# Sinkhorn block attention followed by a token mixer: a staged kernel becomes one software pipeline over batches

## The chip, the core and the metric

The kernel runs on one core of a Trainium2 chip. The core has a matrix engine (PE, whose weight loads the profile lists as PEld), a vector engine (DVE), a scalar engine (ACT), GpSimd (POOL), and a queue engine (SP) that here only issues transfers. PE writes to PSUM alone; DVE and ACT copy from there to the on-chip SBUF; transfers go over 16 DMA engines. The metric is device time in microseconds (us) for one execution; smaller is better.

## The reference

There are 4 batches, 8 heads, 768 tokens, 64 elements a head. An 8 x 8 matrix P for each batch and head is normalised five times (exponential, rows, columns). It mixes the 8 blocks of 96 tokens of K and of V. Then each block of Q attends to the mixed block at its own place. The heads side by side form x, 768 x 512, which goes through a mixer without softmax.

```python
    for _ in range(5):
        P = P - np.max(P, axis=-1, keepdims=True)
        P = np.exp(P)
        P = P / (np.sum(P, axis=-1, keepdims=True) + 1e-09)
        P = P / (np.sum(P, axis=-2, keepdims=True) + 1e-09)
    ...
    k_sorted = np.einsum('bhij,bhjcd->bhicd', P, k_b).reshape(B, H, S, D)
    v_sorted = np.einsum('bhij,bhjcd->bhicd', P, v_b).reshape(B, H, S, D)
    ...
    W_tok = scale * np.einsum('bsd,btd->bst', wq, wk)
    mixed = np.einsum('bst,btd->bsd', W_tok, x)
    return (np.maximum(mixed, 0.0) @ w_out).astype(np.float32)
```

Here wq and wk are x times two 512 x 64 weights. The kernels form wk transposed times x first (64 x 512, "Ab"), then wq times it.

## The kernel before

The instructions of each engine are ordered by the framework's scheduler. The work has three stages.

*Sinkhorn* (lines 59 to 77): 32 matrices on 32 partitions, eight small DVE operations and one exponential on ACT an iteration. P transposed goes to DRAM (L77).

*Two groups of two batches* (loop at L93). A partition is one block of one head, 128 in all, and holds its 96 x 64 elements in one row. Sixteen small transfers (L97) read P back into a block-diagonal 128 x 128 matrix, `lhsT`. Q, K and V come in over POOL's queue with a cast to bf16 (L106, L110). K and V are multiplied by `lhsT`, 512 columns at a time (L113), and copied out of PSUM by ACT (L115) and DVE (L123). PE then transposes Q, K and V in pieces of 128 x 64 or 128 x 96 (L145, L160), up to 32 into one PSUM tile. One copy of up to 4096 elements a partition takes each tile out, reading with a stride (L154, L169). Attention (L172 to L205) takes four heads of a block at a time: four score matmuls (L180), one exponential (L186), four matmuls with V (L190), whose 65th column of ones gives the row sum, a reciprocal (L198) and a product (L205). The result goes to DRAM (L208).

*Mixer* (loop at L232), one batch at a time: x is read back twice, transposed (L236) and plain (L242). Then come wq (L249), wk (L257), Ab (L265), the mixing with ReLU (L274 to L277) and the output product (L283), copied by ACT or DVE (L286) and stored on SP's queue (L287).

Of the kernel before, what the change touches and what calls it, by code (L numbers as in the profile page):

```python
# [17 lines left out]
def kernel(  # L18
# [16 lines left out]
    GRP = 128 // NB  # L35
    NG = BH // GRP
    P = 128
    CD = BLK * D
    scale = 1.0 / math.sqrt(D)

    d_model = moe_w_out.shape[0]
    d_hyper = moe_w_q.shape[1]
    moe_scale = 1.0 / math.sqrt(d_hyper)
    D1 = D + 1

    assert (B, H, S, D) == (4, 8, 768, 64)
    assert NB == 8 and BLK == 96 and d_model == 512 and d_hyper == 64

    dram = ctx.enter_context(tc.tile_pool(name="dram", bufs=1, space=bass.MemoryType.DRAM))
# [4 lines left out]
    id128 = const.tile([P, P], FP32)  # L54
    id128b = const.tile([P, P], BF16)
    make_identity(nc, id128)
    make_identity(nc, id128b)

    with tc.tile_pool(name="sink", bufs=1) as sk:
        Pm = sk.tile([BH, NB, NB], FP32)  # L60
        nc.sync.dma_start(out=Pm, in_=sort_net.rearrange("b h i j -> (b h) i j"))
        tmp = sk.tile([BH, NB, 1], FP32)
        for _ in range(5):
            nc.vector.reduce_max(tmp, Pm, axis=AX.X)
            nc.vector.tensor_sub(Pm, Pm, tmp.to_broadcast([BH, NB, NB]))
            nc.scalar.activation(Pm, Pm, ACT.Exp)
            nc.vector.reduce_sum(tmp, Pm, axis=AX.X)
            nc.vector.reciprocal(tmp, tmp)
            nc.vector.tensor_mul(Pm, Pm, tmp.to_broadcast([BH, NB, NB]))
            Pmt = Pm.transpose([0, 2, 1])  # L70
            nc.vector.reduce_sum(tmp, Pmt, axis=AX.X)
            nc.vector.reciprocal(tmp, tmp)
            tview = tmp.transpose([0, 2, 1]).to_broadcast([BH, NB, NB])
            nc.vector.tensor_mul(Pm, Pm, tview)
        PTs = sk.tile([BH, NB, NB], BF16)
        nc.vector.tensor_copy(PTs, Pm.transpose([0, 2, 1]))
        nc.sync.dma_start(out=PT_dram, in_=PTs)  # L77
# [4 lines left out]

    MM = 512

    with (
        tc.tile_pool(name="gin", bufs=2) as gin,
        tc.tile_pool(name="gbf", bufs=1) as gbf,
        tc.tile_pool(name="gT", bufs=1) as gT,
# [229 lines left out]
```

## Time and profile before

| What | us |
|---|---|
| three runs | 243.16, 245.55, 245.48 |
| median | 245.48 |
| span of the profiled execution (first to last instruction) | 241.4 |
| PE, DVE, ACT busy within it | 163.0, 112.1, 93.8 |
| PEld, POOL busy within it | 110.2, 12.3 |

The page gives no time for the profiled execution but its span; what lies around the span is part of the runs' times. In the views, a line such as L154 is a line of the kernel, an arrow gives what is written and what is read, and "x64" is the number of instructions. The granted clock is the share of PE's clock that was let through, 1.00 at most. A matmul's listed duration overlaps that of the next one, so prices of matmuls are taken from the chain of waits, where a row gives the time that a row of them took.

### The profile page before, as it was taken

The numbers are of one execution on the slowest core, as the hardware profiler recorded it, in microseconds if no ns is written. First come the engines' busy times: TensorE is split into PE (matmuls) and PEld (weight loads), VectorE is DVE, ScalarE is ACT, GpSimd is POOL, SyncE is SP. The second block draws the span as 40 slices with busy tenths as digits, with TensorE's granted clock in tenths as the row PEclk, the third lists the DMA queues.
The fourth block names the chain that finished last, engine by engine and source line by source line (L and its number), as shares of the span: only waits on it lengthen the run. The fifth ranks groups of instructions, "written<-read, shape, count | busy, mean of one in ns | idle before, by whom it ended". The sixth has DMA issues, their size and how long they took to land.

```text
span 241.4 us, 3551 instructions
## 1 busy us (share of the span) xinstructions
PE 163.0 (68%) x1347; PEld 110.2 (46%) x1352; DVE 112.1 (46%) x245; ACT 93.8 (39%) x150; POOL 12.3 (5%) x30
## 2 busy tenths in 40 slices
PE   0000028586672999978685663899997998969783
PEld 0000012286672888863185562688874343333330
DVE  4720003816677445560917766545563244435332
ACT  2100018056541554538126652364541334333340
POOL 4010000000000000010190000000000000000000
PEclk9999999779977555556959999555555899999998
DMA  5829932997900011121072002797321489950615
GB/s 89 173 33 198 220 72 33 218 206 129 200 3 0 18 51 50 55 65 30 0 78 34 0 3 53 191 134 194 107 62 49 91 241 273 231 215 27 234 72 190
DMA packets 26512, 26.06 MB, mean 108 GB/s; under 512 B 16000, under 2 KB 22656, under 8 KB 25728
## 3 DMA queue, kind: packets, MB, share of 16 engines
q1 hardware_dynamic: 23904, 15.75, 24.3%
q0 software_dynamic: 2592, 10.09, 22.3%
q8 instruction: 10, 0.16, 0.3%
q14 instruction: 6, 0.05, 0.1%
HBM read 23.34 MB, written 9.44 MB: 136 GB/s over the span
## 4 chain that ended last, share of the span: by engine, by line
PE 51%; DVE 27%; DMA 10%; ACT 6%; issue 3%; SPq 2%; DVEq 0%; ACTq 0%
PE psS L180 12%; PE psO L190 11%; PE tpqk L145 8%; DVE KT L154 7%; PE ps L283 7%; DMA lhsT<-PT_dram 6%; DVE V_S L123 6%; ACT K_S L115 4%; DVE VT L169 4%; DVE QT L154 4%; PE ps L274 3%; PE ps L249 3%; PE psAb L265 2%; DMA out_dram<-ot 2%; PE tpv L160 2%
## 5 line engine op out<-in xcount | busy, mean ns | idle before, releaser
L186 ACT ACTIVATE E<-psS 96x384 bf16<-96x384 f32 x64 | 30.2, 485 | 35.7 <-PE psS L180 19.9
L180 PE MATMUL psS<-QT,KT 64*96 64x96 bf16 x256 | 33.0, 284 | 9.1 <-DVE VT L169 9.1
L113 PE MATMUL mixps<-kgb,lhsT 128*128 128x512 bf16 x23 | 9.8, 574 | 36.2 <-DMA lhsT<-PT_dram 34.5
L190 PE MATMUL psO<-VT,E 96*96 96x65 bf16 x256 | 32.6, 273 | 1.2 <-DVE xb L205 1.1
L180 PEld LDWEIGHTS <-KT 64*96 64x96 bf16 x256 | 24.4, 183 | 12.8 <-DVE VT L169 9.4
L123 DVE CAST V_S<-mixps 128x512 bf16<-128x512 f32 x24 | 14.5, 684 | 32.1 <-PE mixps L113 32.1
L113 PEld LDWEIGHTS <-lhsT 128*128 128x128 bf16 x48 | 5.4, 115 | 50.7 <-issue 49.0
L190 PEld LDWEIGHTS <-E 96*96 96x96 bf16 x256 | 24.9, 184 | 6.7 <-DVE xb L205 0.8
L283 PE MATMUL ps<-wo,mixT 128*128 128x512 bf16 x92 | 24.1, 380 | 3.4 <-DVE ot L286 2.3
L205 DVE TENSOR_TENSOR xb<-psO,R 96x256 bf16<-96x256 f32 x64 | 23.7, 402 | 2.0 <-DMA x_dram<-xb 1.8
L198 DVE RECIPROCAL R<-psO 96x4 f32<-96x4 f32 x64 | 11.4, 178 | 27.6 <-PE psO L190 25.5
L154 ACT COPY QT<-tpqk 64x4096 bf16<-64x4096 bf16 x4 | 14.3, 3565 | 24.0 <-PE tpqk L145 24.0
L115 ACT CAST K_S<-mixps 128x512 bf16<-128x512 f32 x24 | 11.9, 652 | 26.6 <-PE mixps L113 26.6
L154 DVE COPY KT<-tpqk 64x4096 bf16<-64x4096 bf16 x4 | 17.7, 4417 | 8.6 <-PE tpqk L145 8.6
L145 PE MATMUL tpqk<-id128b,Q_S 128*64 128x128 bf16 x192 | 15.9, 262 | 6.3 <-DVE V_S L123 3.8
L145 PEld LDWEIGHTS <-Q_S 128*64 128x64 bf16 x192 | 15.6, 140 | 8.3 <-issue 8.3
L145 PE MATMUL tpqk<-id128b,K_S 128*64 128x128 bf16 x192 | 12.2, 223 | 7.9 <-DVE KT L154 4.5
L286 DVE COPY ot<-ps 128x512 f32<-128x512 f32 x12 | 8.3, 692 | 16.8 <-DMA out_dram<-ot 7.1
L145 PEld LDWEIGHTS <-K_S 128*64 128x64 bf16 x192 | 11.6, 113 | 8.5 <-issue 8.5
L283 PEld LDWEIGHTS <-mixT 128*128 128x128 bf16 x96 | 7.9, 97 | 15.5 <-issue 9.4
L154 DVE COPY QT<-tpqk 64x4096 bf16<-64x4096 bf16 x2 | 8.8, 4416 | 12.4 <-PE tpqk L145 12.4
L276 DVE TENSOR_SCALAR mixT<-ps 128x384 bf16<-128x384 f32 x16 | 8.9, 554 | 9.3 <-PE ps L274 9.3
(48 smaller groups left out, 144.2 us busy)
## 6 DMA issues: line engine op xcount, KB each, us to landing
out_dram<-ot SPq DMA_DIRECT2D x24, 256.0 KB
Q_S<-in_q_dram POOLq DMA_DIRECT2D x2, 1536.0 KB, 10.5
kgb<-in_k_dram POOLq DMA_DIRECT2D x2, 1536.0 KB, 10.3
vgb<-in_v_dram POOLq DMA_DIRECT2D x2, 1536.0 KB, 14.6
x_dram<-xb SPq DMA_DIRECT2D x32, 96.0 KB
X<-x_dram SPq DMA_DIRECT2D x24, 128.0 KB
lhsT<-PT_dram SPq DMA_DIRECT2D x32, 0.1 KB
wo<-in_moe_w_out_dram POOLq DMA_DIRECT2D x4, 128.0 KB, 3.3
```

What stands on the lines that cost most here:

```text
L113: nc.tensor.matmul(ps, lhsT, ldb[:, t * MM:(t + 1) * MM])
L115: nc.scalar.copy(dst[:, t * MM:(t + 1) * MM], ps)
L123: nc.vector.tensor_copy(ov, iv)
L145: nc.tensor.matmul(ps[:, ci * P:(ci + 1) * P], src[:, c * D:(c + 1) * D], id128b, is_transpose=True, start=(ci % 8 == 0), stop=(ci % 8 == ...
L154: cpeng()(ov, iv)
L169: cpeng()(ov, iv)
L180: nc.tensor.matmul(psS[:, t * BLK:(t + 1) * BLK], KT2[:, p * BLK:(p + 1) * BLK], QT2[:, p * BLK:(p + 1) * BLK], start=(t == 0), stop=(t == 3),
L186: nc.scalar.activation(E, psS, ACT.Exp, scale=scale)
L190: nc.tensor.matmul(psO[:, t * D1:(t + 1) * D1], E[:, t * BLK:(t + 1) * BLK], VT2[:, p * D1:(p + 1) * D1], start=(t == 0), stop=(t == 3), s ...
L198: nc.vector.reciprocal(R, sums)
L205: nc.vector.tensor_mul(dstv, avv, R.to_broadcast([BLK, 4, D]))
L283: nc.tensor.matmul(ps, mixT[pt][:, st * P:(st + 1) * P], wo_t[pt], start=(pt == 0), stop=(pt == PT4 - 1))
```

## The change

The three stages become one loop of 32 steps, step (b, i) being block i of batch b with all eight heads. The program's order is kept as it is written (`manual_schedule`). All PSUM tiles come from one pool of four.

- Nothing goes through DRAM between stages. P is spread over 128 partitions by two small matmuls on PE and a few DVE products (`PBD`, `PTR`).
- K is laid out with six consecutive tokens to a partition. `prep_k` multiplies it by a matrix M made from P instead of by the identity, so that one matmul transposes and mixes; `prep_v` does the same with the block-diagonal `PBD`. `prep_q` only transposes. Q of two heads shares a tile whose other halves are zero (`QZ`), so that one score matmul with 128 rows serves two heads.
- `xt` transposes the attention's result on PE for the mixer.
- Within step (b, i) stand the scores and the exponential of the next step, pieces of pending work, and the product with V of this step. The pending work of batch b is the preparation of b + 1 and, from step 1, the mixer of b - 1. It is dealt out by cost: `work.left() / (NB - 1 - i)` in each step, all of it by step 6.
- Loads: Q and K by batch, V by group, all issued by POOL at the start in the order shown. Each of the mixer's stores takes two of the six token rows of every partition.
- The first Sinkhorn iteration alone takes off the maximum; the small constant of the column sum is a ninth row of the tile.

The core of the diff; all of the old body (lines 35 to 287) goes:

```diff
-    PT_dram = dram.tile([BH, NB, NB], BF16)
-    x_dram = dram.tile([B, S, d_model], BF16)
...
+    ctx.enter_context(tc.manual_schedule())
+    psp = ctx.enter_context(tc.tile_pool(name="ps", bufs=4, space=bass.MemoryType.PSUM))
+    def psum(shape, dtype=FP32):
+        return psp.tile(shape, dtype, tag="ps", name="ps")
...
+    def load_q(b):
+        Qn[b] = inp.tile([P, H, R6, D], BF16, tag="Qn", name="Qn", bufs=3)
+        nc.gpsimd.dma_start(out=Qn[b].rearrange("p h r d -> p h (r d)"),
+                            in_=q[b].rearrange("h (p r) d -> p h (r d)", p=P))
...
+    idb = const.tile([P, P], BF16)
+    make_identity(nc, idb)
+    load_q(0)
+    load_v(0)
+    load_k(0)
...
+    QZ = [const.tile([P, NP, 2, S], BF16, name=f"QZ{n}") for n in range(2)]
+    VT = [const.tile([BLK, P, D1], BF16, name=f"VT{n}") for n in range(NG)]
+    nc.vector.memset(Pm[:, NB:NB + 1, :], 1e-9)
+    for n in range(2):
+        eng = nc.vector if n == 0 else nc.gpsimd
+        eng.memset(QZ[n][0:D, :, 1, :], 0.0)
+        eng.memset(QZ[n][D:P, :, 0, :], 0.0)
+    for g in range(NG):
+        nc.gpsimd.memset(VT[g][:, :, D:D1], 1.0)
...
+    nc.vector.reduce_max(m_j, idb.rearrange("p (h j) -> p j h", j=NB), axis=AX.X)
+    nc.vector.reduce_max(m_h, idb.rearrange("p (h j) -> p h j", j=NB), axis=AX.X)
+    nc.vector.reduce_max(m_p, idb.rearrange("p (j s) -> p s j", s=SP), axis=AX.X)
...
+    nc.gpsimd.tensor_copy(rep, idb[0:BH, 0:BH].unsqueeze(2).to_broadcast([BH, BH, NB]))
+    nc.gpsimd.tensor_copy(L_j, m_j.unsqueeze(2).to_broadcast([P, NB, SP]))
+    load_q(1)
+    load_k(1)
...
+    nc.gpsimd.dma_start(out=wq_t, in_=moe_w_q.rearrange("(t p) d -> p t d", p=P))
+    nc.gpsimd.dma_start(out=wk_t, in_=moe_w_k.rearrange("(t p) d -> p t d", p=P))
+    nc.gpsimd.dma_start(out=wo_t, in_=moe_w_out.rearrange("(t p) d -> p t d", p=P))
+    load_q(2)
+    load_v(1)
+    load_k(2)
+    load_q(3)
+    load_k(3)
...
+    for it in range(5):
+        if it == 0:
+            nc.vector.reduce_max(tmp, Pv, axis=AX.X)
+            nc.vector.tensor_sub(Pv, Pv, rows(tmp))
+        nc.scalar.activation(Pv, Pv, ACT.Exp)
+        nc.vector.reduce_sum(tmp, Pv, axis=AX.X)
+        nc.vector.reciprocal(tmp, tmp)
+        nc.vector.tensor_mul(Pv, Pv, rows(tmp))
+        nc.vector.reduce_sum(tmp, Pm.rearrange("p i j -> p j i"), axis=AX.X)
+        nc.vector.reciprocal(tmp, tmp)
+        nc.vector.tensor_mul(Pv, Pv, cols(tmp))
+    Pb = const.tile([BH, NB, NB], BF16)
+    nc.vector.tensor_copy(Pb, Pv)
...
+    def prep_q(b):
+        QK[b] = [QZ[b % 2], None]
+        for kp in range(NP):
+            ps = psum([P, R6, P], BF16)
+            for r in range(R6):
+                for hh in range(2):
+                    nc.tensor.matmul(ps[hh * D:(hh + 1) * D, r, :], Qn[b][:, 2 * kp + hh, r, :],
+                                     idb, is_transpose=True, start=True, stop=True,
...
+            psf = ps.rearrange("p r s -> p (r s)")
+            nc.vector.tensor_copy(QZ[b % 2][0:D, kp, 0, :], psf[0:D])
+            nc.vector.tensor_copy(QZ[b % 2][D:P, kp, 1, :], psf[D:P])
+            yield 12 * 40
+    def make_m(b):
+        M = rot.tile([P, H, NB, SP], BF16, tag="M", name="M")
+        nc.vector.tensor_mul(
+            M, PTR[:, b * H:(b + 1) * H].unsqueeze(3).to_broadcast([P, H, NB, SP]),
+            m_p.unsqueeze(1).unsqueeze(1).to_broadcast([P, H, NB, SP]))
...
+    def prep_k(b):
...
+        for kp in range(NP):
+            ps = psum([P, 1024])
+            for r in range(R6):
+                for hh in range(2):
+                    h = 2 * kp + hh
+                    nc.tensor.matmul(ps[hh * D:(hh + 1) * D, r * P:(r + 1) * P],
+                                     Kn[b][:, h, r, :],
+                                     M[:, h].rearrange("p i s -> p (i s)"),
+                                     start=True, stop=True, skip_group_check=True)
+            nc.scalar.copy(KT[:, kp], ps[:, 0:S].rearrange("p (r s) -> p s r", r=R6))
...
+    def prep_v(g):
+        for d0 in range(0, D, 8):
+            ps = psum([P, 8, P])
+            for dd in range(8):
+                nc.tensor.matmul(ps[0:BLK, dd, :],
+                                 Vn[g][:, :, d0 + dd],
+                                 PBD[g].rearrange("p h i -> p (h i)"),
+                                 start=True, stop=True, skip_group_check=True)
+            ov = VT[g][:, :, d0:d0 + 8]
+            iv = ps[0:BLK].rearrange("p d n -> p n d")
+            if (d0 // 8) % 2:
+                nc.scalar.copy(ov, iv)
+            else:
+                nc.vector.tensor_copy(ov, iv)
+            yield 8 * 56
+    def scores(b, i):
+        Qz, KT = QK[b]
+        ps = psum([P, 2, 512])
+        for kp in range(NP):
+            nc.tensor.matmul(
+                ps[0:BLK, kp // 2, (kp % 2) * 2 * BLK:(kp % 2 + 1) * 2 * BLK],
+                KT[:, kp, i * SP:(i + 1) * SP].rearrange("p s r -> p (s r)"),
+                Qz[:, kp].rearrange("p w (r s) -> p w r s", r=R6)[:, :, :, i * SP:(i + 1) * SP],
+                start=True, stop=True, skip_group_check=True)
+        E = rot.tile([BLK, H * BLK], BF16, tag="E", name="E", bufs=3)
+        nc.scalar.activation(E.rearrange("p (a n) -> p a n", a=2), ps[0:BLK, :, 0:4 * BLK],
+                             ACT.Exp, scale=scale)
+        return E
+    def av(b, i, E):
+        g, b2 = b // BG, b % BG
+        ps = psum([P, 2, 512])
+        for h in range(H):
+            m = P if h < H - 1 else BLK
+            nc.tensor.matmul(ps[0:m, h // 4, (h % 4) * D1:(h % 4 + 1) * D1],
+                             E[:, h * BLK:h * BLK + m],
+                             VT[g][:, (b2 * H + h) * NB + i, :],
+                             start=True, stop=True, skip_group_check=True)
...
+        nc.vector.reciprocal(Rt, pv[:, :, :, D])
+        nc.vector.tensor_mul(Xb[b][:, i].rearrange("p (a t d) -> p a t d", a=2, t=4),
+                             pv[:, :, :, 0:D],
+                             Rt.unsqueeze(3).to_broadcast([BLK, 2, 4, D]))
+    def xt(b, i0):
+        ps = psum([P, PT, 2 * BLK], BF16)
+        for ii in range(2):
+            for pt in range(PT):
+                nc.tensor.matmul(ps[:, pt, ii * BLK:(ii + 1) * BLK],
+                                 Xb[b][:, i0 + ii, pt * P:(pt + 1) * P], idb[0:BLK, 0:BLK],
+                                 is_transpose=True, start=True, stop=True,
...
+        nc.vector.tensor_copy(XT[b][:, :, i0 * BLK:(i0 + 2) * BLK], ps)
+    def moe(b):
...
+        ps = psum([P, 2, 512])
+        for hh in range(2):
+            for pt in range(PT):
+                nc.tensor.matmul(ps[:, hh, 0:hf],
+                                 wqd[:, pt].rearrange("p a d -> p (a d)"),
+                                 Xt[:, pt, hh * hf:(hh + 1) * hf],
...
+        wqT = rot.tile([P, S], BF16, tag="wqT", name="wqT")
+        nc.scalar.copy(wqT.rearrange("p (a n) -> p a n", a=2), ps[:, :, 0:hf])
+        yield 8 * 163
+        ps = psum([P, NB, DH])
+        for i in range(NB):
+            m = P if i < NB - 1 else BLK
+            for pt in range(PT):
+                nc.tensor.matmul(ps[0:m, i, :], Xt[:, pt, i * BLK:i * BLK + m], wk_t[:, pt, :],
...
+        wkb = rot.tile([BLK, NB, DH], BF16, tag="wkb", name="wkb")
+        nc.vector.tensor_copy(wkb, ps[0:BLK])
+        yield 32 * 40
+        ps = psum([P, DM // 2])
+        for i in range(NB):
+            for a in range(2):
+                nc.tensor.matmul(ps[a * DH:(a + 1) * DH, :], wkb[:, i, :],
+                                 X[:, i, a * 256:(a + 1) * 256],
...
+        Ab = rot.tile([P, DM // 2], BF16, tag="Ab", name="Ab")
+        nc.scalar.mul(Ab, ps, moe_scale)
+        yield 8 * 150
...
+        for p2 in range(2):
+            for hh in range(2):
+                ps = psum([P, 2, 512])
+                for a in range(2):
+                    nc.tensor.matmul(ps[:, a, 0:hf], Ab[a * DH:(a + 1) * DH, p2 * P:(p2 + 1) * P],
+                                     wqv[a * DH:(a + 1) * DH, :, hh * ni:(hh + 1) * ni, :],
...
+                if n % 2:
+                    nc.vector.tensor_relu(ov, iv)
+                else:
+                    nc.scalar.activation(ov, iv, ACT.Relu)
+                n += 1
+                yield 250
+        od = out[b].rearrange("(p r) e -> p r e", r=R6)
+        for r0 in range(0, R6, 2):
+            ps = psum([P, 2, 512])
...
+                    nc.tensor.matmul(ps[:, rr, :], mixT[:, pt, r0 + rr, :], wo_t[:, pt, :],
...
+            if r0 == 2:
+                nc.vector.tensor_copy(ot, ps)
+            else:
+                nc.scalar.copy(ot, ps)
+            nc.sync.dma_start(out=od[:, r0:r0 + 2, :], in_=ot)
+            yield 8 * 216
...
+        def run(self, ns):
+            while ns > 0 and self.gens:
+                try:
+                    c = next(self.gens[0][0])
+                    self.gens[0][1] -= c
+                    ns -= c
+                except StopIteration:
+                    self.gens.pop(0)
...
+    drain(prep_q(0))
+    psv = psum([P, NG, NB, NB])
+    for g in range(NG):
+        nc.tensor.matmul(psv[:, g], rep[:, g * G:(g + 1) * G].rearrange("p h j -> p (h j)"),
+                         Pb, start=True, stop=True, skip_group_check=True)
...
+    for g in range(NG):
+        nc.vector.tensor_mul(pm[:, g], psv[:, g], m_j.unsqueeze(1).to_broadcast([P, NB, NB]))
+    nc.vector.reduce_max(pj, pm, axis=AX.X)
...
+    for g in range(NG):
+        nc.vector.tensor_mul(PBD[g], pj[:, g].unsqueeze(1).to_broadcast([P, G, NB]),
+                             m_h.unsqueeze(2).to_broadcast([P, G, NB]))
+        nc.tensor.matmul(psr[:, g * G:(g + 1) * G], L_j.rearrange("p j s -> p (j s)"), PBD[g],
+                         start=True, stop=True, skip_group_check=True)
+    PTR = const.tile([P, BH, NB], BF16)
+    nc.vector.tensor_copy(PTR, psr)
+    CQ, CK, CV, CM = 4 * 6 * 56, 4 * 12 * 40, 8 * 8 * 56, 8 * 163 + 32 * 40 + 1200 + 1000 + 24 * 216
+    drain(prep_k(0))
+    drain(prep_v(0))
...
+    work = Work()
+    E = scores(0, 0)
+    for n, (b, i) in enumerate(steps):
+        if i == 0:
+            Xb[b] = rot.tile([BLK, NB, DM], BF16, tag="X", name="X")
+            XT[b] = rot.tile([P, PT, S], BF16, tag="XT", name="XT")
+            work.run(1e9)
+            if b + 1 < B:
+                work.add(prep_q(b + 1), CQ)
+                work.add(prep_k(b + 1), CK)
+                if (b + 1) % BG == 0:
+                    work.add(prep_v((b + 1) // BG), CV)
+        if i == 1 and b > 0:
+            work.add(moe(b - 1), CM)
+        if i == NB - 1:
+            work.run(1e9)
+        En = scores(*steps[n + 1]) if n + 1 < len(steps) else None
+        if i % 2 == 0 and i > 0:
+            xt(b, i - 2)
+        if i == 0 and b > 0:
+            xt(b - 1, NB - 2)
+        work.run(work.left() / (NB - 1 - i) if i < NB - 1 else 0)
+        av(b, i, E)
+        E = En
+    xt(B - 1, NB - 2)
+    drain(moe(B - 1))
```

More of the change, by code (lines that the diff above doesn't have):

```diff
@@ L49 @@
-    dram = ctx.enter_context(tc.tile_pool(name="dram", bufs=1, space=bass.MemoryType.DRAM))
-    PT_dram = dram.tile([BH, NB, NB], BF16)
-    x_dram = dram.tile([B, S, d_model], BF16)
+    assert NB == 8 and BLK == 96 and DM == 512 and DH == 64
+    ctx.enter_context(tc.manual_schedule())
     const = ctx.enter_context(tc.tile_pool(name="const", bufs=1))
[L54 to L77, printed above, removed]
```

281 lines of the change are left out of this document (83 added, 198 removed).

## The prediction

> **What bounds the kernel now.** I read the page first, then the chain of waits in order of time, then busy time by stretch, then the groups by form.
>
> ```profile
> span 241.4 us, 3551 instructions
> PEclk9999999779977555556959999555555899999998
> PE 51%; DVE 27%; DMA 10%; ACT 6%; issue 3%; SPq 2%; DVEq 0%; ACTq 0%
> ```
>
> No engine sets the whole end. PE carries half of the chain, DVE a quarter, and the granted clock falls to 5 tenths twice. So the stages follow one another, each with a limit of its own. The stretches show it (PE busy, PEld, DVE, ACT, POOL, then the granted clock, DMA share and GB/s):
>
> ```profile
> 20.00:30.00 10.00, 0.00 (x0) 0.00 (x0) 0.00 (x0) 0.00 (x0) 0.00 (x0) 1.00 1.03 216
> 90.00:100.00 10.00, 10.00 (x89) 8.44 (x87) 5.35 (x22) 5.04 (x11) 0.00 (x0) 0.50 0.18 52
> 140.00:150.00 10.00, 4.81 (x81) 4.47 (x78) 6.91 (x2) 3.87 (x2) 0.00 (x0) 1.00 0.11 21
> 200.00:210.00 10.00, 9.64 (x55) 3.78 (x56) 4.67 (x11) 4.60 (x11) 0.00 (x0) 1.00 0.99 242
> ```
>
> From 20 to 30 us nothing computes: the mixing matrix comes back from DRAM behind the big loads. Around 95 us attention fills PE at half clock. Around 145 us PE waits for copies out of PSUM. Around 205 us the mixer fills PE at full clock. The chain gives the prices (start, duration, what):
>
> ```profile
> 18.95 14.29 DMA lhsT<-PT_dram
> 40.07 7.28 DVE V_S L123 x12
> 47.40 5.88 PE tpqk L145 x64
> 59.81 4.43 DVE KT L154
> 71.23 1.96 PE tpv L160 x32
> 77.70 0.57 PE psS L180 x4
> 93.60 0.48 PE psS L180 x4
> 97.84 0.46 PE psO L190 x4
> 107.31 0.72 DVE xb L205 x2
> 151.99 0.57 PE psS L180 x4
> 182.96 1.47 PE ps L249 x4
> 186.46 0.54 PE ps L257 x8
> 189.66 0.65 PE ps L249 x4
> 196.39 2.70 PE ps L283 x12
> 201.19 0.77 PE psAb L265 x3
> 202.64 0.49 PE ps L274 x2
> 237.38 0.69 DVE ot L286
> ```
>
> The stages are 0 to 77.7 and about 108 to 152 (sort, mix and transposes of one group each), 77.7 to 108 and 152 to 182 (attention), and 182.96 to the end (mixer).
>
> **Prices by element.**
>
> ```profile
> L186 ACT ACTIVATE E<-psS 96x384 bf16<-96x384 f32 x64 | 30.2, 485 | 35.7 <-PE psS L180 19.9 <-PE psO L190 15.8
> L205 DVE TENSOR_TENSOR xb<-psO,R 96x256 bf16<-96x256 f32 x64 | 23.7, 402 | 2.0 <-DMA x_dram<-xb 1.8
> L154 DVE COPY KT<-tpqk 64x4096 bf16<-64x4096 bf16 x4 | 17.7, 4417 | 8.6 <-PE tpqk L145 8.6
> L154 ACT COPY QT<-tpqk 64x4096 bf16<-64x4096 bf16 x4 | 14.3, 3565 | 24.0 <-PE tpqk L145 24.0
> L198 DVE RECIPROCAL R<-psO 96x4 f32<-96x4 f32 x64 | 11.4, 178 | 27.6 <-PE psO L190 25.5
> L286 DVE COPY ot<-ps 128x512 f32<-128x512 f32 x12 | 8.3, 692 | 16.8 <-DMA out_dram<-ot 7.1 <-PE ps L283 5.9 <-PE ps L257 3.9
> ```
>
> DVE: (4417 - 692)/(4096 - 512) = 1.04 ns an element and 160 ns fixed, so 692 ns for 512, 0.96 us for 768, 1.22 us for 1024, 3.35 us for 3072. ACT: (3565 - 485)/(4096 - 384) = 0.83 ns and 166 ns, so 0.80 us for 768 and 1.02 us for 1024. PE at full clock, weight load included: 1.96/32 = 61 ns with 128 columns, 0.54/8 = 67 ns with 64, 0.65/4 = 163 ns with 384, 2.70/12 = 225 ns with 512, 0.77/3 = 257 ns in the accumulation of Ab. At half clock an attention pair is 0.46/4 = 115 ns; 128 columns are 107: of the 64 transposes in 5.88 us, the last 1.28 us ran at full clock (below) and hold 21, so 43 took 4.6.
>
> **What goes.** The two DRAM round trips (PT_dram, x_dram), the separate mix (its 7.28 us of V copies among it), and the 4.43 us copies. The mixing becomes the moving operand of the K and V transposes, X stays on chip, and XT comes from PE transposes. I price the new kernel stage by stage.
>
> **Prologue, DVE in program order.**
>
> ```profile
> 2.47 0.21 DVE L64 TENSOR_REDUCE tmp<-Pm 32x8 f32<-32x64 f32 x1 [2.47 <-DMA Pm<-in_sort_net_dram]
> 4.71 0.21 DVE L64 TENSOR_REDUCE tmp<-Pm 32x8 f32<-32x64 f32 x1
> 0.73 0.20 POOL masks.py:197 MEMSET id<- 128x128 f32 x1 [0.29 <-POOLq L302]
> ```
>
> Two memsets of 3072 elements stand ahead of the Sinkhorn loop: 2 x 3.35 = 6.7 us at the copy's rate (no DVE memset is in the trace; POOL's 128 elements in 0.20 us are at most 1.6 ns an element, the upper end, and 4 us less is my lower end). Three mask reductions, 0.9. An iteration is 4.71 - 2.47 = 2.24 us; four lose the max and the subtraction (about 0.49), so 2.24 + 4 x 1.75 = 9.2, and the cast 0.2. Then prep_q(0): 8 copies x 0.96 = 7.7. Its transposes only need the first load, so they are done long before, into the four PSUM tiles that rotate. The products that spread P, with two matmuls between, about 2.3; make_m (1024 elements) 1.2. From 0.7 this reaches 28.9 us. prep_k(0): 48 matmuls at half clock after an idle PE, 48 x 107 ns = 5.1. prep_v(0): 8 x 0.49 = 3.9 on PE, covered against 4 x 1.22 on DVE beside 4 x 1.02 on ACT. The loop starts at **38 us**.
>
> The loads are off this path while the first K tile lands before 29 us:
>
> ```profile
> Q_S<-in_q_dram POOLq DMA_DIRECT2D x2, 1536.0 KB, 10.5
> q1 hardware_dynamic: 23904, 15.75, 24.3%
> 20.00:21.00 1.00, 0.00 (x0) 1.00 0.99 209
> ```
>
> At 209 GB/s written, 0.79 MB of a Q batch streams in 3.8 us and 1.57 MB of V in 7.5, so with 10.5 - 7.5 = 3 us of latency Q0, V0 and K0 are in by about 20 us. Each row is now cut into runs of 768 bytes. The q1 queue's mean packet of 659 bytes took 0.243 x 16 x 241.4 / 23904 = 39 ns, so 1024 runs over 16 engines cost 2.9 to 5.8 us: no more than 1.5 times the plain rate. POOL issues the second set behind its two memsets (5 to 10 us); the engines are still busy with the first. Nothing is moved past SP's queue: it keeps the first load and the 12 stores.
>
> **Batch 0** (attention 0 with preparation of 1). A step on DVE is reciprocal 0.18 and product 0.69, half an xt copy 0.48, and in steps 0 to 3 one Q piece of two copies, 1.92: 3.27 x 4 = 13.1. PE has 0.36 (scores, 4 x 192 columns) + 0.73 + 0.54 (av, 8 x 67) + 0.25 = 1.9 beside it. Four K steps follow on ACT (0.80 + 0.80) and PE, about 1.9 each: 7.6. Sum **20.7**.
>
> **Batch 1** (plus prep_v(1), mixer 0). Work is dealt by cost/(7 - i). Step 0 takes three Q pieces: 7 copies x 0.96 + 0.87 = 7.6 on DVE. Step 1: Q, make_m, four K, one V: 1.92 + 1.2 + 1.22 + 0.87 = 5.2. Step 2: six V: 3 x 1.22 + 0.96 + 0.87 = 5.5. Then PE leads. The mixer is 8 x 163 + 32 x 67 + 16 x 128 (half of the 257) + 8 x 200 (0.49/2 = 245 with a fill, 163 without) + 24 x 225 ns = 12.5 us. Steps 3 to 6 hold it with 4 x 0.9 of attention, 0.5 of xt, and 2.5 us (my estimate: three handovers of a 692 ns copy and its wait) where wkb, Ab and mixT are awaited: 19.1. Step 7 holds attention alone, 1.7. Sum **39**.
>
> **Batch 2**, no V: 7.6 + 4.5 (five pieces on PE with attention) + 12.5 + 5 x 0.9 + 1.0 + 2.5 + 1.7 = **34**. **Batch 3**, mixer only: 12.5 + 8 x 0.9 + 32 x 61 ns + 2.5 + 1.0 = **25**.
>
> **Tail**: xt 0.96, then the last mixer alone 12.5 with 4 us of uncovered copies, and the last 1.02 us copy with its store (the page's last copy starts at 237.38 and the span ends at 241.4, so 3.3 after it): **21.5**.
>
> Sum 38 + 20.7 + 39 + 34 + 25 + 21.5 = 178 us of span. The page gives 241.4 us of span for the profiled execution; the runs lie from 243.16 to 245.55 with a median of 245.48, so 4 us lie around it. Forecast **182 us**.
>
> **One price in doubt** is that of the dense bf16 copies out of PSUM: 32 of 768 elements in prep_q and 16 in xt. No row has a dense one. The nearest rows, DVE copies from PSUM, give 1.04 ns, so I take that. The low end is half of it, 0.56 us. It saves 8 x 0.4 in the prologue, about 4 in batch 0, 3.5 in batch 1, 3 in batch 2 and under 1 later: some 14 us, so 168. The Trainium skill (VectorE: DVE Perf Modes, "The perf-mode tier table") lets a copy out of PSUM reach two elements a cycle at most, where both sides are 16-bit and dense; by it the sum would be 168, and no row here shows it.
>
> **Rivals.**
>
> *Dense copies at half the price*: 168, worked out above. For it: the copies change from strided to unit step. Against it: no DVE row under 1.04 ns.
>
> *The clock.*
>
> ```profile
> 119.00:119.50 0.50, 0.28 (x2) 1.00 0.00 0
> 120.50:121.00 0.50, 0.00 (x0) 0.50 0.00 0
> 48.50:49.00 0.50, 0.50 (x8) 0.50 0.35 74
> 52.00:52.50 0.50, 0.50 (x13) 1.00 0.46 98
> ```
>
> PE lost the full clock behind the sparse V mix (7.28/12 = 0.61 us for one matmul whose columns stream in 0.22, about 36%) and won it back between 49 and 52 us, in dense transposes. Attention alone never won it: 4 x 96 and 4 x 65 columns in 0.94 us, where 128 took 107 at half clock, is 57%. In the new loop a batch streams about 54,000 columns in 34 to 39 us, at 0.44 ns each some 60 to 70% at full clock and near all of it at half clock, so a dropped clock should come back. Batch 0 and the Q steps (about 40 to 50%) may lose it. The Trainium skill (TensorE: Matmul & The Clock Gate, "Part 4: PE-mode transpose") says that transposes do not count as busy and leave the clock low; the 140 to 150 us row, with nothing but transposes at 1.00, disagrees, and the trace decides. At half clock PE needs in batch 1: attention 8 x (0.64 + 0.92) = 12.5, preparation 160 x 0.107 = 17.1, xt 3.4, mixer 12.5 x 1.85 = 23 (between 115/67 = 1.7 and 1.47/0.65 = 2.3): 56 us, then 49 and 39, against 39, 34 and 25. With half of that: 182 + 23 = 205.
>
> *The other side: the loop stays at half clock throughout.* With 3 us of waits a batch, 26 in batch 0 and 23 + 8.5 in the tail: 40 + 26 + 59 + 52 + 42 + 31 + 4 = 254 us, slower. It takes a window like attention's in every step; the interleaved mixer speaks against it.
>
> *The loads become the bound.* The decisive point is about 2.2 times the plain rate: at 2 times K2 lands at 67 us, just as batch 1 asks for it; at 3 times K0 is 5 us late, Q2 5 more and K2 12 more: about 205. The packet row gives at most 1.5.
>
> **How the numbers follow.** Row-priced sum 0.47 (own range 171 to 195), half-price copies 0.30 (158 to 171), part of the loop at half clock 0.13 (195 to 220), loads 0.05, half clock throughout 0.05. The range 158 to 208 leaves out the half clock throughout, the upper half of the partial one, and a sum with every estimated wait gone (under 158), 0.15 in all. A measurement of this kernel can tell about 1% from no change. Only the fully cold loop ends above 248: slower 0.04, same 0.01, faster 0.95.
>
> **What would show it.** Right: no PE gap of 30 us at the start; a loop start near 38 us with DVE busy throughout before; steps of about 3.3 us in batch 0, DVE-bound; then PE nearly full at clock 1.00 from batch 1's middle to the end; Q copies at 0.96 us (0.56 is the first rival). Wrong: granted clock 0.50 through whole batches; PE waiting for a DMA inside the loop; or more waits of PE for PSUM tiles (four rotate) than the copies explain, each step then being the sum of its engines and not their maximum.

## The result and the profile after

| | before | after |
|---|---|---|
| median (lowest to highest), us | 244.32 (242.53 to 245.55) | 177.44 (176.18 to 179.08) |
| span of the profiled execution, us | 241.4 | 175.0 |
| mean granted clock | 0.805 | 0.858 |

The profiled execution of the changed kernel took 176.88 us, 1.9 more than its span. The ratio is 0.725, with a 95% interval of 0.718 to 0.732. The forecast was 182 and the range 158 to 208. Runs more than 1.5% above the fastest of their kernel count as slow, here and below; the ratios leave them out, and the profiles of xt_late, m_early, all4, all5 and all7 are of slow runs.

From the page of the changed kernel come the busy times, the granted clock in 40 slices and the shares of the chain:

```profile
PE 118.0 (67%) x1373; PEld 91.4 (52%) x1380; DVE 95.1 (54%) x185; ACT 67.8 (39%) x87; POOL 18.2 (10%) x25
...
PEclk9999999555678985855899998589999999987997
...
PE 51%; DVE 38%; issue 4%; ACT 4%; DVEq 0%; ACTq 0%
```

DMA, which held 10% of the chain before, is gone from it. PE's part is unchanged at half, and the rest is now nearly all DVE's. The clock falls in slice 8, is back by slice 14, dips three times up to slice 26 and is nearly full from there on.

The chain of waits of the changed kernel (start, duration, what) gives the ends of the stages:

```profile
1.16 1.34 DVE QZ L96
...
2.86 1.34 DVE QZ L97
...
18.52 0.56 DVE QZ L167
...
21.11 1.24 DVE M L172
22.48 2.77 PE ps L186 x48
25.25 10.69 PE ps L197 x64
...
37.63 0.72 ACT E L219
...
47.42 0.70 DVE X L235
...
57.74 0.70 DVE X L235
...
66.15 2.77 PE ps L186 x48
...
72.92 7.95 PE ps L197 x48
...
101.70 0.70 DVE X L235
...
133.69 0.70 DVE X L235
...
134.78 0.26 PE ps L228 x8
...
136.68 1.01 PE ps L266 x32
...
139.64 1.01 PE ps L274 x16
...
155.08 0.70 DVE X L235
```

L96 and L97 are the memsets, L167 the Q copies, L172 make_m, L186 and L197 the mixing of K and V, L219 the exponential, L235 the product of attention, L228 the matmuls with V, L266 and L274 those of wk and Ab in the mixer. A batch ends with the last L235 product of its eighth step, so the stages can be set beside the forecast:

| stage | forecast | measured | off by |
|---|---|---|---|
| prologue, to the first exponential | 38 | 37.6 | -0.4 |
| batch 0 | 20.7 | 20.8 | +0.1 |
| batch 1 | 39 | 44.0 | +5.0 |
| batch 2 | 34 | 32.0 | -2.0 |
| batch 3 | 25 | 21.4 | -3.6 |
| tail | 21.5 | 19.2 | -2.3 |
| around the span | 4 | 1.9 | -2.1 |

The first two rows look exact, but both are sums of errors that cancel. These are groups by form (line, engine, operation, tiles, shape, count, then busy time and mean ns of one, then idle time before):

```profile
L197 PE MATMUL ps<-PBD,Vn 128*96 128x128 bf16 x128 | 21.9, 360 | 0.0
L197 PEld LDWEIGHTS <-Vn 128*96 128x96 bf16 x128 | 21.3, 257 | 0.3 <-issue 0.3
...
L167 DVE COPY QZ<-ps 64x768 bf16<-64x768 bf16 x16 | 9.0, 561 | 0.2
L247 DVE COPY XT<-ps 128x768 bf16<-128x768 bf16 x16 | 8.9, 558 | 7.3 <-PE ps L243 7.3
...
L172 DVE TENSOR_TENSOR M<-PTR,m_p 128x1024 bf16<-128x1024 bf16 x4 | 4.9, 1221 | 0.1
...
L96 DVE MEMSET QZ<- 64x1536 uint32 x1 | 1.3, 1338 | 0.3 <-issue 0.3
```

A V matmul takes 10.69/64 = 167 ns where 61 was assumed, and its weight load alone 257. The dense copies take 0.56 us where 0.96 was assumed. The memsets take 1.34 where 3.35 was assumed, as 1536 words of 32 bits instead of 3072 elements. The waits of the changed kernel (total us, times, longest) show what PE stood still for:

```profile
PE ps L186 <- DVE M L172: 12.2, 4, 4.5
PE ps L243 <- DVE X L235: 11.7, 16, 1.4
...
PE ps L162 <- DMA Qn<-in_q_dram: 8.9, 1, 8.9
```

PE's only wait for a load is the one for the first Q tile. The two largest waits are inside the loop, but for 1.9 us that PE waits for M in the prologue: the K mixing waits for the mixing matrix, and the transposes of X wait for the product that stands just ahead of them.

### The profile page after: what moved, and what is told of

It is laid out like the page before. It is cut to its first block, busy times and chain, and to the rows that moved or that the text cites. A ratio compares the mean times of both kernels' runs of the same rounds, so it can differ in the third digit from the quotient of the medians.

```text
span 175.0 us, 3173 instructions
## 1 busy us (share of the span) xinstructions
PE 118.0 (67%) x1373; PEld 91.4 (52%) x1380; DVE 95.1 (54%) x185; ACT 67.8 (39%) x87; POOL 18.2 (10%) x25
## 4 chain that ended last, share of the span: by engine, by line
PE 51%; DVE 38%; issue 4%; ACT 4%; DVEq 0%; ACTq 0%
PE ps L197 12%; PE ps L305 11%; DVE X L235 9%; PE ps L186 6%; DVE QZ L167 4%; PE ps L255 4%; DVE QZ L166 4%; DVE mixT L295 4%; PE ps L243 4%; PE ps L228 3%; PE ps L213 3%; DVE M L172 3%; PE ps L266 3%; PE ps L274 2%; DVE R L234 2%
## 5 line engine op out<-in xcount | busy, mean ns | idle before, releaser
L219 ACT ACTIVATE E<-ps 96x768 bf16<-96x768 f32 x32 | 25.5, 807 | 21.1 <-PE ps L213 21.0
L305 PE MATMUL ps<-wo_t,mixT 128*128 128x512 bf16 x89 | 22.0, 379 | 5.9 <-DVE mixT L295 4.8
L235 DVE TENSOR_TENSOR X<-ps,R 96x512 bf16<-96x512 f32 x32 | 22.0, 687 | 1.1
L190 ACT CAST KT<-ps 128x768 bf16<-128x768 f32 x16 | 11.9, 807 | 26.2 <-PE ps L186 26.2
L197 PE MATMUL ps<-PBD,Vn 128*96 128x128 bf16 x128 | 21.9, 360 | 0.0
L197 PEld LDWEIGHTS <-Vn 128*96 128x96 bf16 x128 | 21.3, 257 | 0.3 <-issue 0.3
L213 PE MATMUL ps<-QZ,KT 128*96 128x192 bf16 x128 | 19.2, 282 | 0.9 <-ACT ot L311 0.5
L186 PE MATMUL ps<-M,Kn 128*64 128x128 bf16 x192 | 11.3, 307 | 12.2 <-DVE M L172 12.2
L243 PE MATMUL ps<-idb,X 96*128 96x96 bf16 x128 | 11.6, 216 | 11.8 <-DVE X L235 11.7
L186 PEld LDWEIGHTS <-Kn 128*64 128x64 bf16 x192 | 10.0, 168 | 13.3 <-issue 13.1
L228 PEld LDWEIGHTS <-E 96*128 96x128 bf16 (+1 forms) x256 | 13.4, 111 | 4.6 <-issue 1.4
L228 PE MATMUL ps<-VT,E 96*128 96x65 bf16 (+1 forms) x256 | 15.4, 209 | 0.4 <-ACT E L219 0.4
L213 PEld LDWEIGHTS <-KT 128*96 128x96 bf16 x128 | 13.3, 145 | 1.4 <-issue 0.6
```

The lines of the kernel that those rows point to most:

```text
L186: nc.tensor.matmul(ps[hh * D:(hh + 1) * D, r * P:(r + 1) * P], Kn[b][:, h, r, :], M[:, h].rearrange("p i s -> p (i s)"), start=True, stop= ...
L190: nc.scalar.copy(KT[:, kp], ps[:, 0:S].rearrange("p (r s) -> p s r", r=R6))
L197: nc.tensor.matmul(ps[0:BLK, dd, :], Vn[g][:, :, d0 + dd], PBD[g].rearrange("p h i -> p (h i)"), start=True, stop=True, skip_group_check=True)
L213: nc.tensor.matmul(ps[0:BLK, kp // 2, (kp % 2) * 2 * BLK:(kp % 2 + 1) * 2 * BLK], KT[:, kp, i * SP:(i + 1) * SP].rearrange("p s r -> p (s ...
L219: nc.scalar.activation(E.rearrange("p (a n) -> p a n", a=2), ps[0:BLK, :, 0:4 * BLK], ACT.Exp, scale=scale)
L228: nc.tensor.matmul(ps[0:m, h // 4, (h % 4) * D1:(h % 4 + 1) * D1], E[:, h * BLK:h * BLK + m], VT[g][:, (b2 * H + h) * NB + i, :], start=Tr ...
```

## The experiments

Three suspects came out of these rows: the strided V weights, the place of the X transposes, and the place of make_m. Three other runs ask where the gain comes from, and the rest try to keep it.

**v_dense: V weights from neighbouring elements.** The kernel multiplies other columns of V, so only its time is of use.

```diff
-                                 Vn[g][:, :, d0 + dd],
+                                 Vn[g].rearrange("p c d -> p (c d)")[
+                                     :, (d0 + dd) * BLK:(d0 + dd + 1) * BLK],
```

> The V preparation reads its weights from 96 neighbouring elements instead of every 64th element; its products are of other columns of V, so the output is not the reference's. Theory: the weight load with a stride of 64 elements (257 ns a load) sets 166 ns for each of the 128 matmuls, and a PE that streams only a third of the time then loses its clock. With dense weights 64 matmuls take 3.9 us instead of 10.7 at full clock (6.8 at half clock), twice, and the half clock after V (30 to 47 us, 65 to 69 and 75 to 84 us) goes: 177 falls to 160 to 164 us. Rival: the half clock, not the stride, makes these matmuls slow; then they stay at about 166 ns and the time within 1% of 177. Second rival: the copies out of PSUM (1.22 and 1.19 us) set the pace; then V falls only to about 5 us a group and the time to 167.

Measured: 164.18 us (162.68 to 164.97), ratio 0.667 (0.661 to 0.673), so 13 us less than the change. In its rows of line L197 (count, then shortest, median and longest ns), the weight load has halved; on its chain the first 16 matmuls take 1.41 us, 88 ns each, and then ACT's copies out of PSUM lead:

```profile
L197 PEld LDWEIGHTS <-Vn x128: 120/123/204, 25.2 to 69.3; 128*96 128x96 bf16 x128
```

```profile
25.25 1.41 PE ps L197 x16
...
26.68 4.37 ACT VT L205 x4
```

The theory holds for the time, and the second rival for the pace: with dense weights the first V takes 5.8 us with its last copy, to 31.05, and not 3.9. The strided weights cost 13 us in all. A higher clock behind V is part of that (a mean of 0.93 in this profile, 0.86 in the changed kernel's), and no run takes the two apart. Was the slow V mixing itself due to the clock, which is down in that stretch of the changed kernel? One microsecond of the V mixing (PE and PEld busy with counts, DVE, ACT, POOL, granted clock, DMA share, GB/s), first in the changed kernel, then in m_early below, which mixes the first V in the same way:

```profile
31.00:32.00 1.00, 1.00 (x9) 1.00 (x7) 0.00 (x0) 0.91 (x1) 0.00 (x0) 0.50 1.30 202
```

```profile
31.00:32.00 1.00, 1.00 (x8) 1.00 (x7) 0.00 (x0) 0.88 (x1) 0.00 (x0) 1.00 1.32 205
```

```profile
25.23 10.68 PE ps L199 x64
```

The last row is m_early's chain: 64 matmuls in 10.68 us at full clock, against 10.69 with the clock at half from about 30 us. The load of the weights sets the pace, not the clock.

**xt_late: the X transposes behind the pending work.**

```diff
-        if i % 2 == 0 and i > 0:
-            xt(b, i - 2)
-        if i == 0 and b > 0:
-            xt(b - 1, NB - 2)
         work.run(work.left() / (NB - 1 - i) if i < NB - 1 else 0)
+        if i % 2 == 0 and i > 0:
+            xt(b, i - 2)
+        if i == 0 and b > 0:
+            xt(b - 1, NB - 2)
```

> The transposes of X for the mixer stand behind the pending work of the step instead of right behind the scores. Theory: PE waits 11.7 us in 16 places because the transposes need the product that DVE made just before; behind the pending work that product is done. Where PE sets the step (batches 1 to 3, about 8 us of the waits) the time comes back, in the steps that DVE sets it does not: 177 falls to 168 to 171. Rival: DVE is the bound of most steps, and PE then waits elsewhere for it: 175 to 177.

Measured: 168.0 us (164.66 to 169.01, four runs, too far apart for an interval). In its waits, PE's wait for X is down from 11.7 to 2.9 us; DVE waits for the transposes instead, and the wait for M is as it was:

```profile
DVE XT L247 <- PE ps L243: 13.2, 10, 4.0
PE ps L186 <- DVE M L172: 12.8, 4, 4.5
```

The gain is 9 us by the medians and 11.5 by the fastest run of each, most of the 11.7 that PE waited or all of it. That DVE's new wait costs little is a reading of the total; no run shows it by itself.

**m_early: make_m ahead of the Q copies.** The product that builds M for the next batch is issued at the start of a batch, no longer behind that batch's Q pieces.

```diff
             if b + 1 < B:
+                Ms[b + 1] = make_m(b + 1)
                 work.add(prep_q(b + 1), CQ)
```

> The matrix M for the K preparation of the next batch is made at the start of the batch, ahead of the Q copies on DVE instead of behind them. PE waits for M 12.2 us in 4 places, 1.9 of it in the prologue. Theory: what PE waits for is DVE's whole queue, the Q copies in it, so only the 1.2 us of M itself leave each of the three batches' waits: 177 falls to 173 to 175. Rival: all of the wait is M's place: 167 to 169.

Measured: 165.44 us (165.41 to 168.96), ratio 0.673 (0.668 to 0.678). My expectation failed, and the rival's cause holds: of PE's 12.2 us of waits for M only the 1.9 in the prologue, which the edit leaves alone, remain. The gain of about 12 us is somewhat more than the other 10.3 and than the rival's 8 to 10; where the rest comes from stayed open. Its row of waits, and its chain in batch 1:

```profile
PE ps L188 <- DVE M L172: 1.9, 1, 1.9
```

```profile
55.48 1.13 DVE M L172
...
59.85 0.35 PE ps L188 x12
...
60.23 0.81 ACT KT L192
```

The K mixing starts before 60 us, against 66.15 in the changed kernel. I had thought that K would then only wait for the Q copies. But its pieces are emptied by ACT, so once M is there K depends on DVE only through the four PSUM tiles that all pieces share.

**undealt: all pending work at once.**

```diff
-        work.run(work.left() / (NB - 1 - i) if i < NB - 1 else 0)
+        work.run(1e9)
```

> The pending work is issued in one lump in the step in which it is added, instead of being dealt over steps 0 to 6. Same instructions. Theory: the dealing fills the waits of attention (exponential, product) with PE work; with lumps, preparation and mixer run with their own waits exposed and six or seven steps of each batch run bare, at about 1.7 us instead of 0.9 of PE time: 177 rises by 12 to 25 us. Rival: the order within a batch hardly matters, since the four engines run ahead of each other anyway: within 3 us of 177.

Measured: 178.34 us, ratio 0.725 (0.718 to 0.733), against 0.725 for the change. The rival holds: dealing the work out over the steps is worth nothing that can be measured.

**staged: no interleaving.** Each batch is attention alone, then preparation of the next, then its mixer, with every other part of the new kernel kept.

```diff
-        work.run(work.left() / (NB - 1 - i) if i < NB - 1 else 0)
+        if i == NB - 1 and b + 1 < B:
+            drain(prep_q(b + 1))
+            drain(prep_k(b + 1))
...
+        if i == NB - 1:
+            xt(b, NB - 2)
+            drain(moe(b))
```

> The changed kernel without the interleaving: in each batch the eight steps of attention stand bare, then the preparation of the next batch, the last product with V, the last transpose and the whole mixer. Same instructions, same tiles, nothing through DRAM. Theory: since dealing the work out was worth nothing against one lump, the engines' queues overlap neighbouring stages by themselves, and most of the 67 us gained come from the dataflow on chip, from the steps of eight heads and from the loads ahead, not from the interleaving: 182 to 192 us. Rival: the interleaving carries the gain; then attention bare costs 8 x 1.7 us a batch, the Q and K pieces 8, the mixer 16 and V 11 twice, one after the other: 205 us or more.

Measured: 192.03 us (186.9, 189.67, 194.39, 194.75). Interleaving is worth 10 to 13 us by the two lower runs, taken against 176.9, the median of the change without its highest run; by the medians of all runs it would be 15. The stretch from 80 to 90 us (columns as above) shows what it covers: attention (to 85 us) and the Q pieces behind it keep DVE busy and leave PE at less than half:

```profile
80.00:90.00 10.00, 4.44 (x96) 3.65 (x95) 8.91 (x18) 2.13 (x3) 0.00 (x0) 0.95 0.01 2
```

**old_no_p: the old kernel without its P loads.** Its mixing matrix stays zero, so K and V are multiplied by zeros.

```diff
             for bl in range(GRP):
-                nc.sync.dma_start(
-                    out=lhsT[bl * NB:(bl + 1) * NB, bl * NB:(bl + 1) * NB],
-                    in_=PT_dram[g * GRP + bl],
-                )
```

> The kernel before without the 32 small loads that bring P back from DRAM: its mixing matrix is left at zero, so K and V are mixed with zeros. Theory: the chain of the kernel before waits for these loads until 34.5 us, but the K load would land only some 10 us after its issue at 15.8, and its issue stood behind the store of P; with the loads gone the mix starts with the K tile at about 26 us and the second group is not touched: 245 falls by 8 to 12 us. Rival: the K load itself was held by nothing else and starts at 2 us; then the mix starts at 13 to 18 us: 225 to 229.

Measured: 237.26 us (236.06 to 238.71), ratio 0.974 (0.965 to 0.983), which is 4 to 9 us, about 6.5, a little under what I expected. On its chain another transfer takes the place of the 14.29 us that P took:

```profile
16.24 16.93 DMA vgb<-in_v_dram
...
33.64 7.28 DVE V_S L118 x12
```

The V mix starts at 33.64 instead of 40.07. The store of P stayed in this run, and POOL still issues the K load only behind it, at 15.72 us, so the whole round trip may cost more. Of the 67 us gained, about 6.5 stand for the loads of P and 10 to 13 for the interleaving, if gains found in two different kernels may be set side by side. The rest, nearly 50, comes from what no run took apart: the mixing inside the transposes, the 4.43 us copies that are gone, eight heads in a step, the larger tiles.

**v_copied: V copied on chip into the dense order.** The first V by one ACT copy ahead of the loop, the second by one POOL copy. The two V tiles share one buffer here, so POOL issues the load of the second V, and K and Q behind it, only after the first copy (from 27.25 us on; 16.36 in the changed kernel).

```diff
+    def dense_v(g, copy):
+        Vd[g] = inp.tile([P, D, BLK], BF16, tag="Vd", name="Vd")
+        copy(Vd[g], Vn[g].rearrange("p c d -> p d c"))
+
+    dense_v(0, nc.scalar.copy)
...
-                                 Vn[g][:, :, d0 + dd],
+                                 Vd[g][:, d0 + dd, :],
...
+    dense_v(1, nc.gpsimd.tensor_copy)
```

> The whole computation again, with dense weights for V: each V tile is copied once on chip into an order in which 96 neighbouring elements are one weight, the first by ACT before its K copies, the second by POOL behind its last load. Theory: ACT is idle from 13 to 23 us and its copy of 6144 elements takes 5.3, so the prologue pays little, and POOL is idle after 30 us: 163 to 168 us, as with the dense slice (164.2) and up to 4 more. Rival: POOL's copy is slow (its 256-element copy took 0.62 us, so 6144 take up to 15) and shares a port with DVE, so the second V comes late: 170 to 175.

Measured: 175.89 us (174.67 to 179.49), ratio 0.720 (0.713 to 0.727): nearly nothing gained, even less than the rival's 170 to 175. Two rows of its chain:

```profile
16.33 10.63 ACT Vd L148
...
45.92 9.19 DVE M L179
```

ACT's copy delays the copies of K in the prologue. And M, 1.22 us in the changed kernel, takes 9.19 us. It ends 1 us after the POOL copy, which its row on the timeline puts at 43.53 to 54.01:

```profile
43.53 10.48 POOL L148 COPY Vd<-Vn 128x6144 bf16<-128x6144 bf16 x1 [13.09 <-DMA Vn<-in_v_dram]
```

**all3: v_copied, xt_late and m_early together.** The edits are the three above.

> Dense V weights by copies, the transposes of X behind the pending work, and M made early, together. Theory: the three waits stand in different places (V's matmuls, PE behind the product, PE behind the Q copies), but DVE then carries most steps of batches 0 and 1: of 13 + 9 + 12 us about two thirds add up: 177 falls to 150 to 156. Rival: DVE, busy 94 us, is already the bound of the first half, and the three hide each other: 160 or more.

Measured: **152.06 us** (151.57 to 155.9), ratio 0.623 (0.618 to 0.628), the fastest version tried and inside the range expected. From its page, then from its chain and from POOL's timeline:

```profile
PE 99.2 (66%) x1380; PEld 72.9 (49%) x1380; DVE 96.7 (65%) x185; ACT 77.8 (52%) x88; POOL 28.9 (19%) x26
...
PEclk9999999999999995699999999999999999999997
```

```profile
50.00 4.88 DVE M L179
```

```profile
43.09 10.69 POOL L148 COPY Vd<-Vn 128x6144 bf16<-128x6144 bf16 x1 [12.90 <-DMA Vn<-in_v_dram]
```

PE's busy time fell by 19 us and the clock stays full but for one dip. ACT's copy of V (16.04 to 26.62 us) still leads the prologue, and M is still held up: as in v_copied it ends 1.1 us after POOL's copy. So the next four runs tried to get these back.

**all4, all5, all6, all7: other places for the copy of V.** In all4, ACT copies both V in eight pieces each, the second as pending work of batch 0; its load stands earlier, and Q and K have two buffers each instead of three. In all6, POOL keeps the second copy but in 16 pieces. all5 and all7 are these two with pieces of K and Q issued in turn. The core of each:

```diff
+        for d0 in range(0, D, 8):
+            nc.scalar.copy(Vd[g][:, d0:d0 + 8, :],
+                           Vn[g][:, :, d0:d0 + 8].rearrange("p c d -> p d c"))
+            yield 400
...
+    dense_v(1, nc.gpsimd.tensor_copy, 16)
...
-                work.add(prep_q(b + 1), CQ)
-                work.add(prep_k(b + 1), CK)
+                work.add(both(prep_q(b + 1), prep_k(b + 1)), 8 * 480)
```

> As the three changes together (152.1), but no copy on POOL: ACT copies the first V in eight pieces, four of them behind its K copies, and the second V in eight pieces as pending work of batch 0; its load stands earlier, and Q and K tiles have two buffers instead of three. Theory: POOL's 10.5 us copy held up DVE's product of two SBUF operands (M took 4.9 and 9.2 us instead of 1.2), and ACT's one copy of 10.6 us held the first K copies by 3 us; both go: 145 to 149. Rival: the slow M came from something else than POOL's copy, and ACT becomes the bound of batch 0 (10.6 us more on it): 151 to 155.

> As the kernel beside it, with the K and the Q pieces of the preparation in turn instead of all Q pieces first. Theory: Q pieces are emptied by DVE (1.1 us each) and K pieces by ACT (0.8 us), so in turn both engines work in the same steps and PE waits less for PSUM tiles: 2 to 5 us less than it. Rival: DVE's total is the same and is what the first half of the kernel waits for: within 1 us of it.

> The three changes together (152.1) with POOL's copy of the second V cut into 16 pieces. Theory: DVE's product for M waits for POOL's running copy, 10.5 us as one instruction (M took 4.9 us in that run); with pieces of about 0.7 us it waits for one of them at most, M stays under 2 us, and PE and ACT, which stood behind it from 50 to 58 us, gain 2 to 3.5 us: 148.5 to 150. Rival: DVE loses the port to each next piece in turn, so M is as slow as before: 151.5 to 153.

> As the kernel beside it, with K and Q pieces in turn. Theory: where ACT is not loaded with copies of V in batch 0, the turn lets ACT and DVE empty PSUM in the same steps: 1 to 3 us less than the kernel beside it. Rival: DVE's work in batches 0 to 2 is the bound and its sum is the same: within 1 us.

Measured: all4 158.69 us (ratio 0.642, 0.634 to 0.650); all5 157.56 (152.93 to 158.6, too far apart for an interval); all6 156.01 (0.638, 0.632 to 0.645); all7 154.07 (0.630, 0.625 to 0.634). All are slower than all3 by their medians, though all7's interval overlaps all3's. The theories of all4 and all6 failed, and both took longer than their rivals said too. In all4, a stretch by engine and two groups by form:

```profile
50.00:60.00 10.00, 4.06 (x49) 3.35 (x49) 4.17 (x8) 10.00 (x10) 0.00 (x0) 0.52 0.42 64
```

```profile
L153 ACT COPY Vd<-Vn 128x768 bf16<-128x768 bf16 x16 | 23.0, 1510 | 3.1 <-DMA Vn<-in_v_dram 3.1
...
L184 DVE TENSOR_TENSOR M<-PTR,m_p 128x1024 bf16<-128x1024 bf16 x4 | 4.9, 1214 | 0.0
```

With no POOL copy, M is back at 1.2 us, so that copy is what slowed it. But ACT is now full and the exponentials of attention stand behind 1.5 us pieces. That this is where the time went is my reading; the fewer buffers were not tried alone. In all6, DVE's timeline, and POOL's copies as a group:

```profile
50.54 6.64 DVE L181 TENSOR_TENSOR M<-PTR,m_p 128x1024 bf16<-128x1024 bf16 x1
```

```profile
L149 POOL COPY Vd<-Vn 128x384 bf16<-128x384 bf16 x16 | 12.5, 838 | 13.2 <-DMA Vn<-in_v_dram 13.2
```

M does not slip in between two pieces of 0.84 us: it takes 6.64 us and again ends 1.1 us after the last of them, at 57.18 against 56.10. So the three long durations of M are what was left of POOL's copying when M's turn came, plus about its own 1.2 us. What else makes all6 slower than all3 stayed open. For K and Q in turn, all7 against all6 is 2 us as expected, with intervals that overlap a little; all5 against all4 shows nothing certain.

## Why the prediction was right, and where it was not

**The structure was right in the main.** No gap of 30 us opens the kernel, DVE sets the prologue up to M and the Q steps of batch 0, the loads are hidden, and a dropped clock comes back. The rival of the loads did not occur: PE waits for no load in the loop. Half clock held for parts of the loop, never for a whole batch. Two of the prediction's own signs failed, as three stretches of the changed kernel show (columns as above):

```profile
40.00:50.00 10.00, 6.99 (x86) 5.57 (x82) 8.12 (x16) 2.97 (x4) 0.00 (x0) 0.66 1.22 195
50.00:60.00 10.00, 8.34 (x152) 7.01 (x153) 5.47 (x13) 6.03 (x8) 0.00 (x0) 0.83 0.43 67
...
100.00:110.00 10.00, 4.82 (x96) 3.86 (x95) 8.63 (x16) 3.26 (x4) 0.00 (x0) 0.91 0.13 54
```

PE is not nearly full from the middle of batch 1 on: from 80 to 160 us it is busy for 4.8 to 9.2 of every 10, at a granted clock of 0.75 to 1.00. And DVE bounds only the first half of batch 0. Its four Q steps took 10.5 us (to 48.1) and not 13.1, with the cheaper copies; its four K steps took 10.3 and not 7.6, since PE waits in them for M and for the products. So the forecast of batch 0 was 2.6 too high in one half and 2.7 too low in the other, and that the sum was met is luck.

**The time was right partly by luck.** The step that failed is the price of the V mixing: "8 x 0.49 = 3.9 on PE", from 61 ns a matmul. That price came from the old transposes of V (L160), and their weights are dense, as this row of the kernel before shows (shortest, median, longest ns):

```profile
L160 PEld LDWEIGHTS <-V_S x128: 119/123/204, 66.7 to 147.1; 128*96 128x96 bf16 x128
```

They were dense because DVE had put V into that order in the 7.28 us of copies that the prediction counted among what goes. The change hands this reordering to the weight load: the new weights are 64 elements apart, and the step measured 10.69, an excess of 6.8 in the prologue and about as much in batch 1; v_dense puts the whole at 13 us, with what the clock adds. With dense weights too the 3.9 was short: the copies led, as the prediction's own 4 x 1.22 on DVE would have said. Opposite to it stands the price in doubt: the dense copies cost what the first rival said, 0.56 and not 0.96, which that rival had put at 14 us. The two cancel. With both prices right the sum would have been much the same.

The Trainium skill (Advanced Engine Details and Errata, "SBUF Cachelines") says that on-chip memory is read in lines of 16 bytes and that an access which goes to a new line each time pays a penalty. The trace agrees with it, at 257 ns a load against 123 dense; no run tried a stride in between, so the 16 bytes themselves are not shown. The V weights are 128 bytes apart, so this rule spoke against the step, and the prediction did not use it. The tier table of the Trainium skill (VectorE: DVE Perf Modes) that the prediction cited agrees with the trace, 0.56 us for 768 elements where the strided rows gave 0.96.

**The prologue, term by term.** Memsets 2.7 and not 6.7 (-4.0); eight Q copies 4.5 and not 7.7 (-3.2); the rest up to M +0.6; K mixing 2.77 and not 5.1 (-2.3), because the clock was granted in full there (0.99 from 20 to 30 us); V +6.8; the last V copy and wqd, not priced, +1.7. The sum is -0.4.

**Waits were left out.** The prediction took steps as the maximum of their engines. It charged M its own 1.2 us and xt half a copy. It did not ask who waits for M behind the Q copies (10.3 us of PE in the loop, given back by m_early) or for the product just ahead of xt (11.7, of which xt_late gave back 9 or more). Batch 1 came out 5.0 higher: it holds the second V mixing and a long wait for M. Batch 2 came out lower all the same, since its eight Q copies alone were priced 3.2 us too high. Batch 3 was 3.6 us lower than its sum, and its chain shows terms that were too high: eight matmuls with V take 0.26 us where 0.54 was priced, the 32 of wk 1.01 and not 2.1, the 16 of Ab 1.01 and not 2.05, some 4 us in all. The price of 67 ns for 64 columns, from the 0.54/8 of L257, is about twice what these took. The tail was 2.3 us lower; which of its terms was too high no run took apart. POOL's two memsets, put at 5 to 10 us, took 5.4 together.

**Around the span** lie 1.9 us and not 4. The prediction took the whole distance from the span of before to the median of its runs; with 1.9 the profiled execution of before took about 243.3, which is close to the fastest of the three runs shown and not to their median.

**The dealing by cost** set the steps from which batch 1 was summed. Issued in one lump the kernel runs alike: what matters is that other work is there, not how evenly it is dealt.

## What to carry to other kernels

Price a matmul by the stride of its weights as well as by its columns: take the price from a row whose weights lie in memory in the same way. When a pipeline is written by hand, ask of each instruction who waits for it and what stands ahead of it in its queue; here moving two calls, without any change to the work, gave 9 to 12 and about 12 us. A copy that repairs a layout takes time on some engine, so look first for whose critical instruction it will stand beside.

## What the runs showed of the hardware

- Weights at a stride of 128 bytes: 257 ns a load of 96 columns against 123 dense, and 167 ns from matmul to matmul against 88; the 167 are the same at half and at full clock.
- ACT reading at that stride: 10.63 us for 6144 elements, 1.73 ns each, twice the 0.83 of its copies out of PSUM in the kernel before; no run has a dense copy to set beside it.
- A DVE product of two operands in on-chip memory was held up by a POOL copy beside it: 1.22 us became 9.19, 4.88 and 6.64, each time ending 1.1 us after POOL's copying, and cutting the copy into 16 pieces did not release it. The Trainium skill (SBUF — State Buffer, "Who interferes with whom") says that a DVE instruction with two such inputs contends with a GpSimd instruction that reads this memory; the trace agrees.
- The clock in the V mixing was 0.50 in one execution and 1.00 in another, with the same matmuls at the same pace. What decides it stayed open.

Not tried: a layout of V in DRAM or a load that brings it in dense order without a copy, and a product for M that reads one operand from elsewhere, which might keep DVE clear of POOL's copy.
